# The opening of a one-core layer norm, linear attention and gated MLP kernel: all loads on one queue, wk transposed by DMA, tile 3 by another route

## The chip, the cores and the metric

The kernel runs on one core of a Trainium2 chip. The core has a matrix engine (TensorE, PE in the profile), three engines for elementwise work (VectorE, DVE; ScalarE, ACT; GpSimd, POOL) and an engine that here only issues transfers (SyncE, SP). Sixteen DMA engines move data. The metric is the device time of one execution in microseconds (us); lower is better.

## The reference

The input `x` has 2048 tokens of 512 values. It is normalized per token, goes through a linear attention of 32 heads of 16 and through a gated MLP of width 1792, and both results are added to `x`:

```python
xn = _layernorm(x, axis=-1)                      # (x - mean) / sqrt(var + 1e-5)
# attention
q, k, v = split(xn @ wqkv)                       # 32 heads of 16
pq, pk = q @ w_phi, k @ w_phi                    # per head, 16 x 16
phi = concat(softmax(p), softmax(-p))            # of pq and of pk
num = phi_q @ (phi_k^T v);  den = phi_q . sum(phi_k) + 1e-6
A = (num / den) @ wo
# gated MLP
B = ((xn @ w_gate) * (xn @ w_up)) @ w_down
return x + A + B
```

All arrays are bfloat16.

## The kernel before

The 2048 tokens are 16 tiles of 128 (`NT`), in four groups of four (`GT`). A token is a partition of `xall`; the normalized tile is needed transposed, as `xnT` (512 features in four blocks of 128 partitions, by token). Order on each engine is the order of the program text (`manual_schedule`, L92): an engine runs its instructions in that order and waits at each for its inputs.

**Loads (L75 to L89, L97).** All on SP's queue and in this order: tile 0 of x, tile 1, tiles 2 and 3, `wk` (the k columns of `wqkv`, rows on partitions), the first 256 columns of `wg` and `wu` (two units of the MLP), `wphi`, the next 640 columns of each (five units), tiles 4 to 7, the last 896 columns of each (seven units), tiles 8 to 15, `wd`, `wo`. The v columns `wv` go on ScalarE's own queue (L97), behind a one-element Exp (L96) that brings in the activation table.

**Opening (L328 to L357).** TensorE first runs ten products of zeros (`warm_up(10)`, L304). For tiles 0 to 3 VectorE takes statistics (`ln_sums`, L146) and aggregates them (L338), adds epsilon (L155), GpSimd raises to the power -1/2 (L157), and VectorE applies mean and scale (L162). The statistics of a tile stand ahead of the normalization of the tile before it. `lt(n)` transposes a normalized tile by four TensorE instructions into PSUM (L207), and ScalarE copies it to `xnT` (L208). `vproj(n)` makes the v product of a tile in four 512-wide matmuls (L235) and copies it out (L316); its argument `amid` puts the transposes of the next tile in the middle of it. `wk_transposes` (L217) turns `wk` into `wT2[:, 1]` by 16 TensorE transposes and two ScalarE copies (L222, L223), between the v products of tiles 1, 2 and 3. `make_bd` (L214, GpSimd) multiplies `wphi` by a block mask into `bd`, and `fold` (L229, L231) combines `wT2` and `bd` into `W1k`, the matrix that gives the projected k directly.

**Afterwards.** `ffn(1)` is one unit of the MLP, one of 14 blocks of 128 columns for a group of four token tiles: four `g` matmuls (L272), four `u` matmuls (L276), a ScalarE copy (L279) and a VectorE product (L280). It needs all four tiles of the group in `xnT`. Units are strewn between the other products so that TensorE always has work. The first units of group 0 alternate with the two halves of the fold of `W1k`; then follow the k features of tiles 0 to 3 (`kproj`, L319, which waits for `W1k`), `kv` sums, and the statistics of later tiles, which are put in as chores (`ln_block`, `chore`). The other tiles of `xnT` are transposed by DMA (L196), and the q half `wT2[:, 0]` by one DMA from DRAM (L379). Then comes attention (`attend`) and the output (`fin`).

**Buffers.** PSUM for products is six banks in rotation (`bank`), so a product waits until the bank six allocations earlier is read out. `hpool` has three large buffers, which `wk`, `wT2` and the `hT` of the groups take in turn.

Of the kernel before, what the change touches and what calls it, by code (L numbers as in the profile page):

```python
# [9 lines left out]
F32 = mybir.dt.float32  # L10
# [11 lines left out]
def kernel(  # L22
# [40 lines left out]
    wo = wpool.tile([P, DC, D], BF16)  # L63

    hpool = ctx.enter_context(tc.tile_pool(name="hpool", bufs=3))
    wk = hpool.tile([P, DC, D], BF16, name="wk", tag="h")
    wT2 = hpool.tile([P, 2, DC, D], BF16, name="wT2", tag="h")

    def dma_x(lo, hi):
        nc.sync.dma_start(out=xall[:, lo:hi, :], in_=x_view[:, lo:hi, :])  # L70

    def dma_cols(eng, w, src, lo, hi, at=0):
        eng.dma_start(out=w[:, :, lo - at:hi - at], in_=src[:, lo:hi].rearrange("(c p) f -> p c f", p=P))

    F1, F2 = 2 * P, 7 * P  # L75
    for lo, hi in ((0, 1), (1, 2), (2, 4)):
        dma_x(lo, hi)
    dma_cols(nc.sync, wk, A_wqkv, D, 2 * D, at=D)
    dma_cols(nc.sync, wg, B_w_gate, 0, F1)
    dma_cols(nc.sync, wu, B_w_up, 0, F1)  # L80
    nc.sync.dma_start(out=wphi[:], in_=A_w_phi.rearrange("(c h) d f -> (h d) c f", c=DC))
    dma_cols(nc.sync, wg, B_w_gate, F1, F2)
    dma_cols(nc.sync, wu, B_w_up, F1, F2)
# [10 lines left out]
    nc.vector.memset(zeros[:], 0.0)  # L94
    first = consts.tile([P, 1], BF16)
    nc.scalar.activation(out=first[:], in_=zeros[:, 0:1], func=AF.Exp, scale=1.0)  # L96
    dma_cols(nc.scalar, wv, A_wqkv, 2 * D, 3 * D, at=2 * D)  # L97
    ident = consts.tile([P, P], BF16)
    make_identity(nc, ident[:])
    mhalf = consts.tile([P, GT], F32)  # L100
# [38 lines left out]
    def bank(name, dt=F32, n=TT):  # L139
        return ps_s.tile([P, n], dt, name=name, tag="s")  # L140
# [9 lines left out]
        stats = ln_sums(n)  # L150
        nc.vector.bn_aggr(out=mv, in_=stats[:])

    def ln_rstd(mv, k):
        ve = lnpool.tile([P, GT], F32, name="ve")
        nc.vector.tensor_scalar(out=ve[:, 0:k], in0=mv[:, 0:k, 1], scalar1=EPS, scalar2=None, op0=ALU.add)  # L155
        rstd = lnpool.tile([P, GT], F32, name="rstd", bufs=GT)
        nc.gpsimd.tensor_tensor(out=rstd[:, 0:k], in0=ve[:, 0:k], in1=mhalf[:, 0:k], op=ALU.pow)  # L157
        return rstd

    def ln_apply(n, mean, rstd):  # L160
        xn = xnpool.tile([P, D], BF16, name="xn")
        nc.vector.tensor_scalar(out=xn[:], in0=xall[:, n, :], scalar1=mean, scalar2=rstd,  # L162
                                op0=ALU.subtract, op1=ALU.mult)
        xns[n] = xn

    def mv_tile():
# [10 lines left out]
    def ln_block(lo):  # L177
        mv = mv_tile()
        nb = lnpool.tile([P, GT], F32, name="nb", bufs=GT)
        rstd = []  # L180

        def scales():
            ve = lnpool.tile([P, GT], F32, name="ve4")
            nc.gpsimd.tensor_scalar(out=ve[:], in0=mv[:, :, 1], scalar1=EPS, scalar2=None, op0=ALU.add)
            r = lnpool.tile([P, GT], F32, name="rstd4", bufs=GT)
            nc.gpsimd.tensor_tensor(out=r[:], in0=ve[:], in1=mhalf[:], op=ALU.pow)
            nm = lnpool.tile([P, GT], F32, name="nm")
            nc.gpsimd.tensor_scalar(out=nm[:], in0=mv[:, :, 0], scalar1=-1.0, scalar2=None, op0=ALU.mult)
            nc.gpsimd.tensor_tensor(out=nb[:], in0=nm[:], in1=r[:], op=ALU.mult)
            rstd.append(r)  # L190

        def apply(i):
            xn = xnpool.tile([P, D], BF16, name="xn")
            nc.scalar.activation(out=xn[:], in_=xall[:, lo + i, :], func=AF.Identity,
                                 scale=rstd[0][:, i:i + 1], bias=nb[:, i:i + 1])
            nc.sync.dma_start(out=xnT[:, :, (lo + i) * P:(lo + i + 1) * P], in_=xn[:], transpose=True)  # L196

        for i in range(GT):
            chores.append(lambda i=i: ln_stats(lo + i, mv[:, i, :]))
        chores.append(scales)  # L200
        for i in range(GT):
            chores.append(lambda i=i: apply(i))

    def lt(n):
        tp = bank("tp", BF16).rearrange("p (c t) -> p c t", c=DC)
        for c in range(DC):
            nc.tensor.transpose(out=tp[:, c, :], in_=xns[n][:, c * P:(c + 1) * P], identity=ident[:])  # L207
        nc.scalar.copy(out=xnT[:, :, n * P:(n + 1) * P], in_=tp)  # L208

    bd = consts.tile([P, DC, 8, DH], BF16)  # L210

    def make_bd():
        bo, wp = BO[:], wphi[:]
        nc.gpsimd.tensor_tensor(out=bd[:], in0=_bcast_ap(bo, [bo.ap[0], [0, DC], [E1, 8], [1, DH]]),  # L214
                                in1=_bcast_ap(wp, [wp.ap[0], [DH, DC], [0, 8], [1, DH]]), op=ALU.mult)

    def wk_transposes(jp):  # L217
        tp = bank("tp", BF16, 2 * TT).rearrange("p (c t) -> p c t", c=DC)
        for i in range(2):
            j = jp * 2 + i  # L220
            for c in range(DC):
                nc.tensor.transpose(out=tp[:, c, i * P:(i + 1) * P], in_=wk[:, j, c * P:(c + 1) * P], identity=ident[:])  # L222
        nc.scalar.copy(out=wT2[:, 1, :, jp * 2 * P:(jp + 1) * 2 * P], in_=tp)  # L223

    def fold(qk, dst, js, copy=nc.scalar.copy):
        for j in js:
# [73 lines left out]
    def warm_up(k):  # L300
        for _ in range(k):
            nc.tensor.matmul(warm, lhsT=zeros[:, 0:P], rhs=zeros[:], start=True, stop=True)
# [3 lines left out]
    with tc.tile_pool(name="ps_k", bufs=1, space=PSUM) as ps_k:  # L306
        kvps = [ps_k.tile([P, 4, 4, E1], F32, name=f"kv{b}") for b in range(2)]
        phiks = {}

        def vproj(n, copy=nc.scalar.copy, amid=None):  # L310
            ps = bank("pv")
            proj(ps, n, wv, range(2))
            if amid is not None:
                amid()
            proj(ps, n, wv, range(2, DC))
            copy(out=vts[n % NV][:, :, :, 0:DH], in_=ps.rearrange("p (a b c) -> p a b c", a=8, b=4))  # L316

        def kproj(n):
            phiks[n] = features(n, W1k, "k")  # L319

        def kv(n):
            vt, phik = vts[n % NV], phiks[n]
            for gr in range(NG):
                nc.tensor.matmul(kvps[gr // 4][:, gr % 4, :, :].rearrange("p a b -> p (a b)"),  # L324
                                 lhsT=phik[:, gr, :], rhs=vt[:, gr, :, :].rearrange("p a b -> p (a b)"),
                                 start=(n == 0 and gr % 4 == 0), stop=(n == NT - 1 and gr % 4 == 3))

        mvs = [mv_tile() for n in range(GT)]  # L328
        rstds = []

        def first_apply(n):
            ln_apply(n, mvs[n][:, 0, 0:1], rstds[n][:, 0:1])

        for n in range(GT):
            stats = ln_sums(n)
            if n > 0:
                first_apply(n - 1)
            nc.vector.bn_aggr(out=mvs[n][:, 0, :], in_=stats[:])  # L338
            rstds.append(ln_rstd(mvs[n], 1))
        first_apply(GT - 1)  # L340
        make_bd()
        nc.gpsimd.tensor_tensor(out=M4[:], in0=BO[:, 0:4, :], in1=BO[:, 4:8, :], op=ALU.add)
        lt(0)
        warm_up(2)
        vproj(0, amid=lambda: lt(1))
        vproj(1, copy=nc.vector.tensor_copy, amid=lambda: lt(2))
        wk_transposes(0)
        vproj(2, copy=nc.vector.tensor_copy, amid=lambda: lt(3))
        wk_transposes(1)
        vproj(3, copy=nc.vector.tensor_copy)  # L350
        ffn(1)
        fold(1, W1k, (0, 1))
        ffn(1)
        fold(1, W1k, (2, 3))
        ffn(1)
        ln_block(4)
        ffn(1)  # L357
        chore(2)
        kproj(0)
        ffn(1)  # L360
        chore(2)
        ffn(1)
        chore()
        kproj(1)
        ffn(1)
        chore()
        ffn(1)
        kproj(2)
        chore()
        ffn(1)  # L370
        kv(0)
        chore()
        ffn(1)
        kproj(3)
        chore()
        ffn(1)
        kv(1)
        ffn(1)
        nc.sync.dma_start(out=wT2[:, 0, :, :], in_=A_wqkv[:, 0:D], transpose=True)  # L379
        for n in range(GT, NT):  # L380
            if n in (4, 8):
                ln_block(n + 4)
            vproj(n)
            kproj(n)
            chore(1 if n % GT < 2 else 0)
            ffn(1)
            kv(n - 2)
            chore((1, 2, 2, 2)[n % GT])
            if n >= 8 and n % 2 == 0:
                qproj((n - 8) // 2)  # L390
            if n == 6:
                fold(0, W1q, (0, 1))
            ffn(1)
            if n == 6:
                fold(0, W1q, (2, 3))
        ffn(1)
        kv(NT - 2)
        ffn(1)
        kv(NT - 1)
        for b in range(2):  # L400
            nc.vector.tensor_tensor(out=KV[:, 4 * b:4 * b + 4, :, :], in0=kvps[b][:],
                                    in1=_bcast_ap(M4[:], [M4[:].ap[0], [0, 4], [E1, 4], [1, E1]]), op=ALU.mult)
        qproj(4)
        ffn(1)
# [64 lines left out]
```

## Time and profile before

| what | value |
|---|---|
| median of 3 runs | 225.01 us (224.81 to 225.06) |
| profiled execution, its own time | 224.9 us |
| profiled execution, span from first to last instruction | 223.2 us |
| first v product starts (L235) | 6.33 us |
| four v products of tile 3 start | 12.05 us |
| first `g` product of the MLP starts (L272) | 12.93 us |
| VectorE idle before statistics, waiting for x | 2.2 us in 2 waits |
| last large load (`wo`) lands | 12.45 + 18.1 = 30.6 us |

Times inside the profile count from the start of the span. A timeline row gives start, length, engine, line, operation, the tile written and the tiles read, and, where the engine stood idle before, how long and for what. Some rows of the opening before:

```profile
2.99 0.69 DVE L146 BATCH_NORM_STATS2 stats<-xall 128x6 f32<-128x512 bf16 x1 [1.11 <-DMA xall<-in_A_x_dram]
...
4.79 0.41 DVE L162 TENSOR_SCALAR xn<-xall,mv,rstd 128x512 bf16<-128x512 bf16 x1
...
5.69 0.59 ACT L208 COPY xnT<-tp 128x512 bf16<-128x512 bf16 x1 [3.41 <-PE tp L207]
...
6.33 0.60 PE L235 MATMUL pv<-wv,xnT 128*128 128x512 bf16 x2 [0.25 <-ACT xnT L208]
6.61 0.69 DVE L146 BATCH_NORM_STATS2 stats<-xall 128x6 f32<-128x512 bf16 x1 [1.13 <-DMA xall<-in_A_x_dram]
```

The first column is the start, so ScalarE had been idle for 3.41 us when it copied the first transposed tile at 5.69, and VectorE waited 1.13 us for tiles 2 and 3 of x, until 6.61.

### The profile page before, as it was taken

To read this page: it belongs to the slowest core of one execution; us is meant where nothing else is said; L and a number is where in the kernel's file an instruction comes from. 1 tells how busy PE (TensorE), PEld (TensorE's weight loads), DVE (VectorE), ACT (ScalarE), POOL (GpSimd) and SP (SyncE) were. 2 spreads that over 40 slices of the span, in tenths; PEclk is the share of its full clock that TensorE was granted. 3 is DMA by queue.
4 is the path that set the end of the run, shared out by engine and by line. 5 is a ranking of instruction groups with operands and counts; after the bars stand their busy time and mean duration, and the time that the engine had idled before them with its cause. 6 is when DMAs were issued, how large, how long until landed. Compare 5 with 4: busy or idle time off the path is not lost.

```text
span 223.2 us, 3437 instructions
## 1 busy us (share of the span) xinstructions
PE 217.4 (97%) x1278; PEld 105.4 (47%) x1278; DVE 137.9 (62%) x237; ACT 90.3 (40%) x161; POOL 72.1 (32%) x59
## 2 busy tenths in 40 slices
PE   7799999999999999999999999999999999999994
PEld 2354444445444444444454444444444444444453
DVE  5634986586559875757679975097745746444321
ACT  2574575448955685646354122222222222100000
POOL 3310455336235663636315453014033033000000
PEclk9999999999999999999999999999999999999999
DMA  6999923501110224020203664314431431622301
GB/s 178 317 381 394 349 55 74 94 1 21 38 38 0 47 50 94 1 47 3 47 1 71 99 140 94 75 24 94 94 73 24 93 72 24 91 55 71 72 25 47
DMA packets 44481, 19.91 MB, mean 89 GB/s; under 512 B 35248, under 2 KB 44080, under 8 KB 44336
## 3 DMA queue, kind: packets, MB, share of 16 engines
q1 hardware_dynamic: 43936, 19.16, 34.8%
q10 hardware_dynamic: 528, 0.52, 0.8%
q8 instruction: 10, 0.16, 0.3%
q14 instruction: 7, 0.06, 0.1%
HBM read 9.19 MB, written 2.10 MB: 51 GB/s over the span
## 4 chain that ended last, share of the span: by engine, by line
PE 95%; DMA 2%; DVE 1%; SPq 0%; ACT 0%; issue 0%
PE fin L288 22%; PE u L276 22%; PE g L272 22%; PE fin L291 6%; PE k L235 6%; PE q L235 6%; PE pv L235 6%; DMA xall<-in_A_x_dram 2%; PE ab L412 2%; PE kv L324 2%; PE pq L229 1%; PE tp L222 0%; PE tp L207 0%; SPq L70 0%; DVE stats L146 0%; ACT xnT L208 0%
## 5 line engine op out<-in xcount | busy, mean ns | idle before, releaser
L276 PE MATMUL u<-xnT,wu 128*128 128x512 bf16 x224 | 57.5, 379 | 0.0
L272 PE MATMUL g<-xnT,wg 128*128 128x512 bf16 x224 | 57.5, 379 | 0.0
L280 DVE TENSOR_TENSOR hT<-u,g_sb 128x512 bf16<-128x512 f32 x56 | 37.1, 668 | 28.3 <-PE u L276 19.5
L247 DVE TENSOR_REDUCE sums<-e 128x64 f32<-128x1024 f32 x32 | 38.9, 1215 | 21.5 <-ACT e L244 21.5
L279 ACT CAST g_sb<-g 128x512 bf16<-128x512 f32 x56 | 32.9, 588 | 46.5 <-PE g L272 46.5
L288 PE MATMUL fin<-wd,hT 128*128 128x512 bf16 (+1 forms) x238 | 51.1, 366 | 0.0
L251 POOL TENSOR_TENSOR phiq<-e,rs 128x1024 bf16<-128x1024 f32 x16 | 30.9, 1932 | 61.5 <-DVE rs L249 53.2
L251 POOL TENSOR_TENSOR phik<-e,rs 128x1024 bf16<-128x1024 f32 x16 | 30.9, 1932 | 47.6 <-DVE rs L249 45.6
L276 PEld LDWEIGHTS <-wu 128*128 128x128 bf16 x224 | 21.9, 98 | 26.4
L288 PEld LDWEIGHTS <-hT 128*128 128x128 bf16 x238 | 23.0, 98 | 24.1
L272 PEld LDWEIGHTS <-wg 128*128 128x128 bf16 x224 | 21.1, 98 | 23.4
L235 PEld LDWEIGHTS <-xnT 128*128 128x128 bf16 x192 | 17.2, 97 | 18.7 <-ACT xnT L208 1.7
L294 DVE TENSOR_TENSOR o_sb<-fin,xall 128x512 bf16<-128x512 f32 (+1 forms) x17 | 11.2, 656 | 22.4 <-PE fin L291 22.4
L243 ACT ACTIVATE e<-q 128x512 f32<-128x512 f32 x16 | 9.5, 596 | 26.1 <-PE q L235 26.1
L249 DVE RECIPROCAL rs<-sums 128x64 f32<-128x64 f32 x32 | 17.7, 553 | 3.1
L235 PE MATMUL pv<-wv,xnT 128*128 128x512 bf16 x64 | 16.9, 379 | 0.6 <-ACT xnT L208 0.5
L291 PE MATMUL fin<-wo,oT 128*128 128x512 bf16 (+1 forms) x68 | 16.6, 366 | 0.0
L235 PE MATMUL k<-W1k,xnT 128*128 128x512 bf16 x64 | 16.4, 379 | 0.0
L235 PE MATMUL q<-W1q,xnT 128*128 128x512 bf16 x64 | 16.4, 378 | 0.0
L243 ACT ACTIVATE e<-k 128x512 f32<-128x512 f32 x16 | 9.6, 597 | 7.0 <-PE k L235 7.0
L316 ACT CAST vt<-pv 128x512 bf16<-128x512 f32 x13 | 7.7, 591 | 11.5 <-PE pv L235 11.5
L146 DVE BATCH_NORM_STATS2 stats<-xall 128x6 f32<-128x512 bf16 x16 | 10.7, 670 | 2.2 <-DMA xall<-in_A_x_dram 2.2
(50 smaller groups left out, 125.1 us busy)
## 6 DMA issues: line engine op xcount, KB each, us to landing
out_dram<-o_sb SPq DMA_DIRECT2D x15, 128.0 KB, 1.9
wd<-in_B_w_down_dram SPq DMA_DIRECT2D x1, 1792.0 KB, 17.5
xall<-in_A_x_dram SPq DMA_DIRECT2D x1, 1024.0 KB, 13.4
wg<-in_B_w_gate_dram SPq DMA_DIRECT2D x1, 896.0 KB, 8.5
wu<-in_B_w_up_dram SPq DMA_DIRECT2D x1, 896.0 KB, 11.4
wg<-in_B_w_gate_dram SPq DMA_DIRECT2D x1, 640.0 KB, 7.9
wu<-in_B_w_up_dram SPq DMA_DIRECT2D x1, 640.0 KB, 7.0
wv<-in_A_wqkv_dram ACTq DMA_DIRECT2D x1, 512.0 KB, 4.4
```

The source lines that it names most:

```text
L235: nc.tensor.matmul(ps, lhsT=xnT[:, j, n * P:(n + 1) * P], rhs=w[:, j, :], start=(j == 0), stop=(j == DC - 1))
L243: nc.scalar.activation(out=e[:, :, 0, :], in_=pfv, func=AF.Exp, scale=1.0)
L247: nc.vector.tensor_reduce(out=sums[:], in_=ev, axis=AX.X, op=ALU.add)
L249: nc.vector.reciprocal(out=rs[:].rearrange("p a b -> p (a b)"), in_=sums[:])
L251: nc.gpsimd.tensor_tensor(out=phi[:].rearrange("p g (x f) -> p (g x) f", f=DH), in0=ev, in1=rs[:].to_broadcast((P, 2 * H, DH)), op=ALU.mult)
L272: nc.tensor.matmul(gps, lhsT=wg[:, c, f * P:(f + 1) * P], rhs=xnT[:, c, T * TT:(T + 1) * TT], start=(c == 0), stop=(c == DC - 1))
L276: nc.tensor.matmul(ups, lhsT=wu[:, c, f * P:(f + 1) * P], rhs=xnT[:, c, T * TT:(T + 1) * TT], start=(c == 0), stop=(c == DC - 1))
L279: nc.scalar.copy(out=g_sb[:], in_=gps)
L280: nc.vector.tensor_tensor(out=hTs[T][:, f, :], in0=ups, in1=g_sb[:], op=ALU.mult)
L288: nc.tensor.matmul(ps, lhsT=hTs[T][:, f, t4 * P:(t4 + 1) * P], rhs=wd[:, f, lo:lo + w], start=(f == 0), stop=False)
L291: nc.tensor.matmul(ps, lhsT=oTs[n][:, c, :], rhs=wo[:, c, lo:lo + w], start=False, stop=(c == DC - 1))
L294: nc.vector.tensor_tensor(out=o_sb[:], in0=ps, in1=xall[:, n, lo:lo + w], op=ALU.add)
```

## The change

- **Loads.** Tiles 1, 2 and 3 of x come in one transfer behind tile 0. `wv` follows on SP's queue; ScalarE issues no transfer any more. Behind the first `wg` and `wu` columns stands one transposing DMA from DRAM that writes `wT2[:, 1]`. `wk`, its tile, its 16 TensorE transposes and their copies are gone.
- **Layer norm of tile 3.** ScalarE sums the tile (Identity with a sum output), GpSimd makes the negative mean, ScalarE sums the squared deviations (Square with a bias and a sum output), and GpSimd makes variance plus epsilon and the power. VectorE only applies them, ahead of tile 2.
- **Copies of tiles 0 and 1 to `xnT`** are made in two halves each. The two warm-up products after `lt(0)` are gone.
- **Order on TensorE.** v products of tiles 0, 1, 3, 2, then two units of the MLP, the first half of the fold, one unit, the second half, one unit. Before, a unit stood ahead of each half and two behind. From the second unit behind the fold on the order is as before.
- `ln_rstd` takes the engine for the addition of epsilon as an argument, and the later layer norm blocks use it with GpSimd, with the same operations as before.

```diff
     hpool = ctx.enter_context(tc.tile_pool(name="hpool", bufs=3))
-    wk = hpool.tile([P, DC, D], BF16, name="wk", tag="h")
     wT2 = hpool.tile([P, 2, DC, D], BF16, name="wT2", tag="h")
...
-    for lo, hi in ((0, 1), (1, 2), (2, 4)):
-        dma_x(lo, hi)
-    dma_cols(nc.sync, wk, A_wqkv, D, 2 * D, at=D)
+    dma_x(0, 1)
+    dma_x(1, 4)
+    dma_cols(nc.sync, wv, A_wqkv, 2 * D, 3 * D, at=2 * D)
     dma_cols(nc.sync, wg, B_w_gate, 0, F1)
     dma_cols(nc.sync, wu, B_w_up, 0, F1)
+    nc.sync.dma_start(out=wT2[:, 1, :, :], in_=A_wqkv[:, D:2 * D], transpose=True)
     nc.sync.dma_start(out=wphi[:], in_=A_w_phi.rearrange("(c h) d f -> (h d) c f", c=DC))
...
-    dma_cols(nc.scalar, wv, A_wqkv, 2 * D, 3 * D, at=2 * D)
...
-    def lt(n):
+    def lt(n, parts=1):
...
-        nc.scalar.copy(out=xnT[:, :, n * P:(n + 1) * P], in_=tp)
+        for c in range(0, DC, DC // parts):
+            nc.scalar.copy(out=xnT[:, c:c + DC // parts, n * P:(n + 1) * P], in_=tp[:, c:c + DC // parts, :])
...
-        for n in range(GT):
-            stats = ln_sums(n)
-            if n > 0:
-                first_apply(n - 1)
-            nc.vector.bn_aggr(out=mvs[n][:, 0, :], in_=stats[:])
-            rstds.append(ln_rstd(mvs[n], 1))
-        first_apply(GT - 1)
+        def first_rstd(n):
+            rstds[n] = ln_rstd(nc.vector, mvs[n], 1)
+        def first_aggr(n, stats):
+            nc.vector.bn_aggr(out=mvs[n][:, 0, :], in_=stats[:])
+            first_rstd(n)
+        last = GT - 1
...
+        nc.scalar.activation(out=junk[:], in_=xall[:, last, :], func=AF.Identity, accum_out=tot[:, 0:1])
+        nmean = lnpool.tile([P, 1], F32, name="nmean")
+        first_aggr(0, ln_sums(0))
+        st = ln_sums(1)
+        nc.gpsimd.tensor_scalar(out=nmean[:], in0=tot[:, 0:1], scalar1=-1.0 / D, scalar2=None, op0=ALU.mult)
+        nc.scalar.activation(out=junk[:], in_=xall[:, last, :], func=AF.Square, bias=nmean[:], accum_out=tot[:, 1:2])
+        first_apply(0)
+        first_aggr(1, st)
+        st = ln_sums(2)
+        first_apply(1)
+        nc.gpsimd.tensor_scalar(out=ml[:, 0, 1:2], in0=tot[:, 1:2], scalar1=1.0 / D, scalar2=EPS,
+                                op0=ALU.mult, op1=ALU.add)
+        rl = lnpool.tile([P, 1], F32, name="rl")
+        nc.gpsimd.tensor_tensor(out=rl[:], in0=ml[:, 0, 1:2], in1=mhalf[:, 0:1], op=ALU.pow)
+        first_aggr(2, st)
+        ln_apply(last, nmean[:], rl[:], op0=ALU.add)
+        first_apply(2)
...
-        lt(0)
-        warm_up(2)
-        vproj(0, amid=lambda: lt(1))
-        vproj(1, copy=nc.vector.tensor_copy, amid=lambda: lt(2))
-        wk_transposes(0)
-        vproj(2, copy=nc.vector.tensor_copy, amid=lambda: lt(3))
-        wk_transposes(1)
-        vproj(3, copy=nc.vector.tensor_copy)
-        ffn(1)
+        lt(0, parts=2)
+        vproj(0, amid=lambda: lt(1, parts=2))
+        vproj(1, copy=nc.vector.tensor_copy, amid=lambda: lt(3))
+        vproj(3, copy=nc.vector.tensor_copy, amid=lambda: lt(2))
+        vproj(2, copy=nc.vector.tensor_copy)
+        ffn(2)
         fold(1, W1k, (0, 1))
         ffn(1)
         fold(1, W1k, (2, 3))
-        ffn(1)
         ln_block(4)
         ffn(1)
```

More of the change, by code (lines that the diff above doesn't have):

```diff
@@ L151, in ln_stats, with ln_rstd @@
         nc.vector.bn_aggr(out=mv, in_=stats[:])
-    def ln_rstd(mv, k):
+    def ln_rstd(eng, mv, k):
         ve = lnpool.tile([P, GT], F32, name="ve")
-        nc.vector.tensor_scalar(out=ve[:, 0:k], in0=mv[:, 0:k, 1], scalar1=EPS, scalar2=None, op0=ALU.add)
+        eng.tensor_scalar(out=ve[:, 0:k], in0=mv[:, 0:k, 1], scalar1=EPS, scalar2=None, op0=ALU.add)
         rstd = lnpool.tile([P, GT], F32, name="rstd", bufs=GT)
@@ L158, in ln_rstd, with ln_apply @@
         return rstd
-    def ln_apply(n, mean, rstd):
+    def ln_apply(n, mean, rstd, op0=ALU.subtract):
         xn = xnpool.tile([P, D], BF16, name="xn")
         nc.vector.tensor_scalar(out=xn[:], in0=xall[:, n, :], scalar1=mean, scalar2=rstd,
-                                op0=ALU.subtract, op1=ALU.mult)
+                                op0=op0, op1=ALU.mult)
         xns[n] = xn
@@ L182, in scales @@
         def scales():
[L183 to L186, printed above, removed]
+            r = ln_rstd(nc.gpsimd, mv, GT)
             nm = lnpool.tile([P, GT], F32, name="nm")
@@ L215, in make_bd @@
                                 in1=_bcast_ap(wp, [wp.ap[0], [DH, DC], [0, 8], [1, DH]]), op=ALU.mult)
[L217 to L223, printed above, removed]
     def fold(qk, dst, js, copy=nc.scalar.copy):
@@ L328 @@
         mvs = [mv_tile() for n in range(GT)]
-        rstds = []
+        rstds = {}
         def first_apply(n):
             ln_apply(n, mvs[n][:, 0, 0:1], rstds[n][:, 0:1])
-        for n in range(GT):
-            stats = ln_sums(n)
-            if n > 0:
-                first_apply(n - 1)
+        def first_rstd(n):
+            rstds[n] = ln_rstd(nc.vector, mvs[n], 1)
+        def first_aggr(n, stats):
             nc.vector.bn_aggr(out=mvs[n][:, 0, :], in_=stats[:])
-            rstds.append(ln_rstd(mvs[n], 1))
@@ L340 @@
-        first_apply(GT - 1)
+            first_rstd(n)
+        last = GT - 1
+        junk = lnpool.tile([P, D], BF16, name="junk")
+        tot = lnpool.tile([P, 2], F32, name="tot")
+        ml = mvs[last]
+        nc.scalar.activation(out=junk[:], in_=xall[:, last, :], func=AF.Identity, accum_out=tot[:, 0:1])
[3 more added lines that the diff above has]
+        nc.gpsimd.tensor_scalar(out=nmean[:], in0=tot[:, 0:1], scalar1=-1.0 / D, scalar2=None, op0=ALU.mult)
```

## Prediction

> **What bounds the kernel.** First the page: busy shares, the slices, the chain that ended last.
>
> ```profile
> PE 217.4 (97%) x1278; PEld 105.4 (47%) x1278; DVE 137.9 (62%) x237; ACT 90.3 (40%) x161; POOL 72.1 (32%) x59
> ...
> PE   7799999999999999999999999999999999999994
> ...
> PE 95%; DMA 2%; DVE 1%; SPq 0%; ACT 0%; issue 0%
> ```
>
> TensorE sets the end. Next the busy time by stretches (us: busy and count of PE, PEld, DVE, ACT, POOL, clock, DMA share, GB/s), cut where the first gated unit's first product starts, 12.93.
>
> ```profile
> 1.24:12.93 11.69, 10.28 (x61) 4.61 (x62) 6.93 (x23) 5.67 (x9) 4.59 (x10) 1.00 0.97 293
> 12.93:215.00 202.07, 202.03 (x1179) 96.89 (x1178) 129.11 (x209) 84.18 (x153) 66.98 (x44) 1.00 0.34 80
> ```
>
> From 12.93 to 215 TensorE idles 0.04 us in 202, so what happens before 12.93 moves the end one for one, and nothing later takes it back unless a new wait appears. The edits all lie before; the mark is the start of that product. Now the chain of waits in time order (start, length, what).
>
> ```profile
> 1.71 4.88 DMA xall<-in_A_x_dram
> ...
> 6.61 0.69 DVE stats L146
> 7.31 0.33 DVE xn L162
> ...
> 8.11 0.59 ACT xnT L208
> ...
> 8.75 0.60 PE pv L235 x2
> ...
> 10.01 0.45 PE tp L222 x8
> ...
> 11.55 0.46 PE tp L222 x8
> 12.01 0.04 issue
> 12.05 1.04 PE pv L235 x4
> ```
>
> The opening hangs on the load of tiles 2 and 3, which lands at 1.71+4.88=6.59. VectorE's statistics of tile 2 start then, and tile 1's normalization stands behind them on VectorE. After that TensorE is nearly full, and 0.45+0.46=0.91 us of it is the 16 transposes of `wk`.
>
> **Loads.** Landing is issue start plus the median to landing: x0 0.79+2.2=2.99, x1 1.25+2.4=3.65, `wv` on ACT's queue 1.22+4.4=5.62, `wk` 8.48, first `wg`/`wu` columns 9.35 and 10.4, `wphi` 10.69, second `wg`/`wu` columns 12.35 and 14.13. The DMA view:
>
> ```profile
> wk<-in_A_wqkv_dram SPq DMA_DIRECT2D x1, 512.0 KB, 6.3
> ...
> wT<-in_A_wqkv_dram SPq DMA_TRANSPOSE x1, 4.4
> ```
>
> Tiles 1 to 3 are now one load of 384 KB issued at 1.25, with only x0 ahead. It can't land before x1 alone did (3.65) nor after 6.59, by when x0 to x3 and `wv` had all landed. By 1-us stretches, 246, 481, 811 and 1095 KB had moved by 3, 4, 5 and 6 us; its last byte is the 524th KB, at 4.15, and x0 landed 0.5 after its last byte. I take L=4.5. `wv` is then third on SP, the 1049th KB, at 5.85 plus lag; the same bytes had landed by 6.59 before. I take 6.5, later than 5.62.
>
> **VectorE, ScalarE, GpSimd.** Tile 3's statistics, aggregate and epsilon leave VectorE (0.69+0.18+0.15=1.02 us). ScalarE gets two passes over tile 3. None with a sum output is in the trace; the rows are 0.59 (128x512 copy) and 0.82 (128x512 with scale and bias tiles), so 0.7 and 0.75, with 0.2 more for reading each sum as upper bound. If Square needed a second table load, that is the 1.28 row; I give it nothing, since copies, Identity and Exp already share the one load. GpSimd gets two small operations at 0.24 and a power at 0.55.
> Step by step with L=4.5. VectorE: tile 1 statistics 4.5 to 5.2, and tile 0's normalization behind them 5.2 to 5.6 (it ran at 4.79; this is a loss); aggregate, epsilon, power, statistics of tile 2 (0.18, 0.15, 0.56, 0.69), tile 1 normalized by 7.15 against 7.62. ScalarE: Identity 4.5 to 5.2, GpSimd's mean to 5.5, Square to 6.3. Tile 0's transposes end at 6.05, but their copies wait behind Square: first half at 6.35. Half copies: 1024 columns took 1.01 and 512 took 0.59, so 256 about 0.38; the first product of tile 0 starts at 6.75 against 6.33. Two warm-up matmuls (0.43) leave, in a time in which TensorE waits anyway.
> What is queued: behind Square all later ScalarE copies; on GpSimd tile 1's power behind the mean (free at 5.5, its input comes at 6.0) and tile 2's behind tile 3's (done 7.5, input 7.55), so no loss; then the mask product `bd`.
>
> **TensorE.** A 512-wide product costs 0.216 (0.86 for four), a tile's four transposes 0.22, and 0.17 passes before their result is whole. Tile 0 first half 6.75; tile 1's transposes 7.2 (input 7.15); tile 0 second half to 7.85; tile 1 from 8.0; tile 3's transposes 8.45 (its normalization 7.6 to 8.0); tile 1 done 9.1. ScalarE: tile 1's copies 7.63 to 8.3, cast of tile 0's values to 8.87, tile 3's copy to 9.46. Tile 3 first half 9.5, tile 2's transposes 9.94, second half to 10.6, tile 2's copy to 10.95, its four products 11.0 to 11.86. No `wk` transposes stand between, nor their 1.01 copies, of which the last held `pv` until 12.05. The first gated product starts at about 11.9 against 12.93: **1.0 us earlier**. Of it 0.9 is the `wk` work. The late start (0.4) is repaid by tiles 2 and 3 coming 2 us earlier, and TensorE still waits some 0.4 twice, on the copies of tiles 3 and 2.
>
> **Is the cover there afterwards?** Two units now stand ahead of the first fold, one between the folds. Unit 2 starts 3.89 after the mark (3.46 of two units, 0.43 of a fold): `wg` columns needed at 15.8, `wu` at 16.7, `wT2` and `bd` at 15.4. The transposed load replaces 512 KB that took 8.48-6.59=1.9. Its other half, alone later:
>
> ```profile
> 39.00:40.00 1.00, 1.00 (x6) 0.42 (x5) 0.47 (x1) 0.43 (x1) 1.00 (x1) 1.00 0.74 101
> 40.00:41.00 1.00, 1.00 (x6) 0.48 (x5) 0.00 (x0) 0.66 (x3) 0.10 (x1) 1.00 1.05 143
> 41.00:42.00 1.00, 1.00 (x8) 0.43 (x6) 0.39 (x1) 1.00 (x3) 0.00 (x0) 1.00 1.25 281
> ```
>
> Those three columns move 525 KB in 3 us with the engines full, some 175 GB/s. Bounds for its time in the queue, T: 1.9 (as plain) and 4.4 (issue to landing alone); I take 3.0, for it starts with descriptors ready. Then everything behind lands 1.1 later than before: `wT2` 8.5+3.0=11.5, `wphi` 11.8, `bd` (1.08) 12.9, second `wg` 13.5, second `wu` 15.2. Slack is 1.5 at the tightest, so I cost the transfer at nothing; at 4.4 `wu` lands at 16.6, still just in time. Its issue holds SP 2.30 instead of 0.43, which puts `wphi`'s issue near 5.7 and the next near 6.3. The latter stood blocked until 7.09 before, so the queue does not run dry. Next on SP are the `xnT` transposes at 30.07; SP was free at 22.46. Tiles 4 to 7 land about 16.6, wanted at about 19.7. `W1k` casts (1.07 for two) have one unit, 1.73, before the first `k` product instead of two: enough.
>
> The Trainium skill, "Advanced Engine Details and Errata", X-Bar Transpose, says that such transfers are as fast as ordinary ones, at 350 to 400 GB/s; the rows above give 175. By the page T would be an estimated 1.4 and the second `wu` would land near 13.6; the total is the same. Against dropping the warm-up stands "TensorE: Matmul & The Clock Gate", Part 1 and Part 4: the array falls to half rate after an idle window of some 3.4 us, and transposes do not count fully as work. Warm-up weight loads here come every 0.43 until 4.5 and products every 0.216 after, and a gap of 0.74 at 6.93 did no harm; the new stretch without a plain product, 5.14 to 6.75, is half a window, so by the page also no fall.
>
> **Sum.** 1.0 off the profiled 224.9 (span 223.2 and 1.7 around it) is 223.9; off the median, 225.0-1.0=**224.0**. With everything else fixed the mark moves one for one with L: L=4.0 gives 223.5, L=5.0 224.5; the 0.2 for each sum output adds up to 0.4 more.
>
> **Rivals.**
> *Gain eaten in the opening* (16%). L near 5.3 (tile 0's normalization waits for all of x), or sum outputs at 0.2 each with `wv` near 7. The mark comes at 12.5 to 12.9: 224.6 to 225.0. For it: two things on the path do start later. Against: the bytes by 4.15.
> *The transposed load is slow in a full queue* (10%), the slower side. `wu`'s second columns land at 14.13-1.9+T. Before, unit 2 ended at 18.98 with both folds done; now 0.86 of products and 0.43 of fold follow the landing. So it decides from T=18.98-1.29-12.23=5.5 on. At T=6.5, 175 GB/s halved and a bit, the end moves to 226.0. For it: nearly all of the page's 35248 packets under 512 B are those of transposes. Against: 4.4 alone, issue included.
> *Half clock returns* (5%). 0.43 instead of 0.216 a product adds 2.2 over eight products and eight transposes (1.73+0.44), of which the two later waits hide 0.9: 224.0+1.3=225.3.
> *The forecast* (69%): 223.5 to 224.5.
>
> A measurement of this kernel can tell 0.2%, 0.45 us, from no change. The forecast with the upper edge taken off, and a little of the first rival, gives faster 0.69; same 0.17; slower 0.14. The range reaches from L=3.7 (223.2) past the eaten gain to 225.2.
>
> **What would show it.** Right: tile 1's statistics start at 4.2 to 4.9, the first `pv` product at 6.5 to 7.1, the first gated product at 11.5 to 12.4, and no wait on TensorE after it. Wrong: statistics after 5.3; an ACT table load beside Square; waits of the fold or of unit 2 for a DMA; products every 0.43 after 6.7.

## The result and the profile after

| what | before | after |
|---|---|---|
| median, 20 runs each | 225.05 us (224.81 to 225.45) | 225.93 us (224.64 to 226.28) |
| ratio, 95% interval | 1 | 1.0024 (1.0014 to 1.0035) |
| profiled execution, time / span | 224.9 / 223.2 us | 225.95 / 224.2 us |
| first `g` product of the MLP | 12.93 us | 14.03 us |

The changed kernel is slower, by 0.24% by the ratio and by 0.39% by the medians. Its 20 times fall into two groups with nothing between: six from 224.64 to 224.82 (middle 224.77) and fourteen from 225.70 to 226.28 (middle 225.96), 1.2 us apart. The kernel before has one group. The profiled execution of the changed kernel belongs to the upper one. All of its loss is made before the first gated product: that starts 1.10 later, and the span is 1.0 longer.

The page of the changed kernel, the lines that answer to those of before, and the granted clock in 40 slices of 5.6 us:

```profile
PE 216.4 (96%) x1236; PEld 105.0 (47%) x1260; DVE 137.0 (61%) x234; ACT 90.0 (40%) x165; POOL 72.7 (32%) x61
...
PEclk9799999999999999999999999999999999999999
...
PE 94%; DMA 2%; ACT 1%; issue 1%; DVE 0%; SPq 0%; POOL 0%
```

The second slice has a clock of 0.7. (TensorE shows 24 matmul records fewer than weight loads; those are records missing from the trace.) Busy time by stretches, in the columns of the prediction's table (busy and count of PE, PEld, DVE, ACT, POOL, then clock, DMA share, GB/s), shows where the clock fell. The changed kernel:

```profile
4.84:8.25 3.41, 1.35 (x9) 0.46 (x8) 2.51 (x8) 2.07 (x6) 1.48 (x4) 1.00 1.24 301
8.25:11.66 3.41, 3.41 (x16) 1.54 (x14) 0.83 (x2) 1.82 (x4) 0.93 (x3) 0.50 0.93 157
11.66:14.20 2.54, 2.29 (x14) 1.03 (x14) 1.39 (x2) 0.59 (x1) 1.06 (x2) 1.00 1.00 344
```

The same stretches before:

```profile
4.84:8.25 3.41, 2.30 (x16) 0.79 (x14) 2.21 (x8) 0.72 (x2) 0.83 (x2) 1.00 1.02 328
8.25:11.66 3.41, 3.16 (x31) 1.96 (x30) 2.00 (x7) 2.69 (x5) 1.71 (x3) 1.00 1.13 317
```

For 3.41 us TensorE ran at half rate, after a stretch of the same length in which it had been busy for 1.35. All of the half-rate stretch counts as busy, so the busy share does not show the loss. Now the chain of waits in time order:

```profile
1.25 4.25 DMA xall<-in_A_x_dram
...
5.52 0.73 ACT junk L334 x2
...
6.33 0.30 POOL nmean L339
...
6.66 0.81 ACT junk L340 x2
7.47 0.27 ACT xnT L205
...
7.79 0.63 PE pv L224 x2
...
8.84 1.71 PE pv L224 x4
...
10.97 1.28 PE pv L224 x4
...
12.52 0.59 ACT xnT L205
...
13.16 1.04 PE pv L224 x4
14.20 0.86 PE g L261 x4
```

Two things differ from what was foreseen. The load of tiles 1 to 3 lands at 5.50, and the chain hangs on it through ScalarE's two passes. And four v products take 1.71 (0.43 each) and not 0.86. The loads of the changed kernel (KB, us from issue to landing):

```profile
wv<-in_A_wqkv_dram SPq DMA_DIRECT2D x1, 512.0 KB, 5.9
...
xall<-in_A_x_dram SPq DMA_DIRECT2D x1, 384.0 KB, 4.2
...
wT<-in_A_wqkv_dram SPq DMA_TRANSPOSE x1, 7.7
```

`wv` lands at 1.71+5.9=7.6, the transposed weights at 3.28+7.7=11.0, which is 1.75 behind the first `wu` columns (2.73+6.5=9.23). TensorE waits for no load afterwards.

### The profile page after: what moved, and what is told of

It is laid out like the page before. It is cut to its first block, busy times and chain, and to the rows that moved or that the text cites. A ratio compares the mean times of both kernels' runs of the same rounds, so it can differ in the third digit from the quotient of the medians.

```text
span 224.2 us, 3380 instructions
## 1 busy us (share of the span) xinstructions
PE 216.4 (96%) x1236; PEld 105.0 (47%) x1260; DVE 137.0 (61%) x234; ACT 90.0 (40%) x165; POOL 72.7 (32%) x61
## 4 chain that ended last, share of the span: by engine, by line
PE 94%; DMA 2%; ACT 1%; issue 1%; DVE 0%; SPq 0%; POOL 0%
PE g L261 22%; PE u L265 21%; PE fin L277 21%; PE pv L224 7%; PE fin L280 6%; PE q L224 6%; PE k L224 6%; PE kv L313 2%; DMA xall<-in_A_x_dram 2%; PE ab L419 2%; PE pq L218 1%; PE tp L203 0%; ACT xnT L205 0%; ACT junk L340 0%; ACT junk L334 0%
## 5 line engine op out<-in xcount | busy, mean ns | idle before, releaser
L265 PE MATMUL u<-xnT,wu 128*128 128x512 bf16 x220 | 56.8, 379 | 0.1
L224 PE MATMUL pv<-wv,xnT 128*128 128x512 bf16 x62 | 17.7, 404 | 1.1 <-ACT xnT L205 1.0
L305 ACT CAST vt<-pv 128x512 bf16<-128x512 f32 x13 | 7.7, 591 | 11.5 <-PE pv L224 11.5
L145 DVE BATCH_NORM_STATS2 stats<-xall 128x6 f32<-128x512 bf16 x15 | 10.0, 668 | 2.5 <-DMA xall<-in_A_x_dram 2.5
```

What stands on the lines that cost most here:

```text
L224: nc.tensor.matmul(ps, lhsT=xnT[:, j, n * P:(n + 1) * P], rhs=w[:, j, :], start=(j == 0), stop=(j == DC - 1))
L265: nc.tensor.matmul(ups, lhsT=wu[:, c, f * P:(f + 1) * P], rhs=xnT[:, c, T * TT:(T + 1) * TT], start=(c == 0), stop=(c == DC - 1))
```

## The experiments

Each was run in five rounds beside the kernel before (medians 225.07 to 225.10 there). Edits are against the changed kernel unless it says otherwise.

**1. Warm-up products in the gaps**

```diff
-    warm_up(10)
+    warm_up(14)
...
         lt(0, parts=2)
+        warm_up(3)
         vproj(0, amid=lambda: lt(1, parts=2))
```

> Four more warm-up products ahead of tile 0's transposes and three behind them; nothing else differs from the changed kernel. Theory (half clock): the clock stays at 1.00 from 8.2 to 11.7, the two groups of times of the changed kernel (224.6 to 224.8 and 225.7 to 226.3) become one, at 224.6 to 224.9. Rival (the late x alone costs the time and the clock record means nothing): no difference, median 225.9. Third case: the products added get in the way of tile 0's transposes, 225 to 225.3, in one group.

Measured: 224.84 (224.71 to 225.16, 11 runs), ratio to before 0.9989 (0.9981 to 0.9998). One group, at the height of the lower one, as the theory had it. The two stretches with this edit:

```profile
4.84:8.25 3.41, 3.41 (x14) 1.30 (x13) 2.50 (x8) 2.17 (x6) 1.80 (x5) 1.00 1.24 306
8.25:11.66 3.41, 3.13 (x23) 1.49 (x22) 1.52 (x3) 1.73 (x5) 0.60 (x3) 1.00 0.91 156
```

Filling the first stretch keeps the clock in the second, although the added products compute nothing that is used. In the second stretch 23 matmuls of the same program started where 16 had. So the upper group is the clock, and it costs 225.96-224.77=1.2 us. (Nine of its fourteen runs list a mean clock of 0.990 to 0.992 and five 1.00; for those five it is inferred from the time.) The late x by itself makes the kernel no slower than before. The products can also be too many: in this profiled execution (225.16, the slowest of the eleven) x landed at 5.45, but the fourteen warm-up products, all at half rate, held tile 0's transposes until 7.18, and the first gated product came 7.78 behind x.

**2. x in three loads, and 3. `wv` on ScalarE's queue**

```diff
-    dma_x(1, 4)
+    dma_x(1, 2)
+    dma_x(2, 4)
```

> The changed kernel with x again as tile 0, tile 1, tiles 2 and 3; wv stays on SyncE's queue. Theory (the one 384 KB load is what comes late): tile 1's statistics start at 4.0 instead of 5.52, tile 0 is normalized near 4.8, TensorE's gap closes by itself and the clock holds; the wait moves to wv, which lands near 7.6; about 224.2. Rival (one queue fills slower than two whatever the pieces are): tile 1 comes by 4.3 but tiles 2 and 3 still at 5.5, and the gain is under 0.5: 225.4 or above, clock lost in some executions.

```diff
-    dma_cols(nc.sync, wv, A_wqkv, 2 * D, 3 * D, at=2 * D)
...
+    dma_cols(nc.scalar, wv, A_wqkv, 2 * D, 3 * D, at=2 * D)
```

> The changed kernel with wv on ScalarE's queue as before; x stays in two loads. Theory (384 KB in one piece is late): tiles 1 to 3 land no earlier than 5.5, later if wv takes half of the engines (to 6.5), and the time stays at 225.9 or goes to 226.5. Rival (two queues are what makes the first microseconds fast): they land by 5.0 and the time falls to 224.7 or below.

Measured: experiment 2 gave 225.29, scattered from 224.37 to 228.05 (12 runs). Tile 0 was normalized at 5.09 as hoped, but tiles 2 and 3 came at 5.56, the first product waited for `wv` until 8.1, and in the profiled execution (227.21) the products still came every 0.43 at 11.5:

```profile
1.24 4.45 PE L292 MATMUL warm<-zeros 128*128 128x512 bf16 x10 [1.24 <-DVE zeros L95]
...
9.33 1.91 PE L225 MATMUL pv<-wv,xnT 128*128 128x512 bf16 x4
...
11.46 1.92 PE L225 MATMUL pv<-wv,xnT 128*128 128x512 bf16 x4
```

Here the rate did not fall: the warm-up products come every 0.43 as well, and the full rate came only after 13 (the four transposes at 13.18 still took 0.63, against 0.39 at the full rate). The execution lists a mean clock of 1.00 all the same, so a listed 1.00 does not prove the full rate. With this in part of the runs, the experiment does not decide between its two cases; experiment 8 takes it up again. Experiment 3 gave 227.08 (226.57 to 227.49, 4 runs), above what either case gave: tiles 1 to 3 landed at 6.12 and `wv` at 1.22+6.3=7.5, and the clock fell too. So two queues do not bring the 384 KB piece sooner: from 3 to 5 us more bytes moved than in the changed kernel (412 against 367 KB), and x still came later. The rival there fell.

**4. The transposed weights alone, in the kernel before**

```diff
-    dma_cols(nc.sync, wk, A_wqkv, D, 2 * D, at=D)
...
+    nc.sync.dma_start(out=wT2[:, 1, :, :], in_=A_wqkv[:, D:2 * D], transpose=True)
...
-        wk_transposes(0)
...
-        wk_transposes(1)
```

> The kernel before with one part of the change alone: the k half of wT2 by transposing DMA in the same place as in the changed kernel, no wk and no transposes on TensorE. Theory (the loss is in the loads and the clock, the transposed load itself is sound): the first gated product comes 0.8 to 0.9 earlier, 224.1 to 224.3. Rival (a transposing load in a full queue holds up what is behind it): TensorE waits for a weight load in the units behind the fold, 225.0 or above.

Measured: 225.03 (224.60 to 225.60, 11 runs), ratio 0.9997 (0.9988 to 1.0005). Both expectations fail: nothing is gained, and no unit waits for a weight load. The timeline of this kernel shows why (start, length, and in brackets the idle time before and its releaser):

```profile
10.17 0.41 DVE L161 TENSOR_SCALAR xn<-xall,mv,rstd 128x512 bf16<-128x512 bf16 x1 [0.67 <-POOL rstd L156]
...
10.95 0.39 PE L206 MATMUL tp<-ident,xn 128*128 128x128 bf16 x4
...
11.37 0.59 ACT L207 COPY xnT<-tp 128x512 bf16<-128x512 bf16 x1 [0.92 <-PE tp L206]
...
12.01 1.04 PE L226 MATMUL pv<-wv,xnT 128*128 128x512 bf16 x4 [0.25 <-ACT xnT L207]
```

Tile 3 is normalized at 10.17, and with no `wk` work left its products still start at 12.01, against 12.05 before. The layer norm chain behind tiles 2 and 3 was as long as TensorE's work; the 0.91 us of transposes lay in the chain of waits with another chain close beside it. A part is the load: tiles 2 and 3 came at 6.86 in this execution, 0.25 later than before, and from there to the products of tile 3 it took 5.15 against 5.44. With x at the old time some 0.3 of the 0.91 would have shown, an estimate from these two executions.

**5. The transposed weights issued later** (with the warm-up products of experiment 1)

```diff
-    nc.sync.dma_start(out=wT2[:, 1, :, :], in_=A_wqkv[:, D:2 * D], transpose=True)
...
     dma_cols(nc.sync, wg, B_w_gate, F1, F2)
+    nc.sync.dma_start(out=wT2[:, 1, :, :], in_=A_wqkv[:, D:2 * D], transpose=True)
```

> The changed kernel with the seven extra warm-up products (so that the clock holds) and with the transposing load issued behind the second wg columns instead of ahead of wphi. Theory (starting that load empties the engines for about 1 us, between 3.0 and 4.0, while x is still coming): no dip of the rate below 190 GB/s between 3 and 5, tiles 1 to 3 land by 4.9 instead of 5.5, the first gated product 0.5 to 0.7 earlier than with the load in its place, 224.2 to 224.4. Rival (one queue with 3 KB rows is slow by itself): the dip stays, x at 5.4 or later, 224.8.

Measured: 224.87 (224.74 to 225.08, 11 runs). The theory falls and the rival's three signs are there: the dip, x after 5.4, and 224.8 to 224.9. The rates by stretches, first of the changed kernel, then of this one:

```profile
3.00:4.00 1.00, 1.00 (x4) 0.38 (x3) 0.93 (x3) 0.00 (x0) 0.00 (x0) 1.00 0.69 132
4.00:5.00 1.00, 1.00 (x4) 0.30 (x2) 0.06 (x1) 0.00 (x0) 0.58 (x1) 1.00 0.91 235
```

```profile
3.00:4.00 1.00, 1.00 (x4) 0.37 (x3) 0.83 (x2) 0.00 (x0) 0.00 (x0) 1.00 0.63 152
4.00:5.00 1.00, 1.00 (x4) 0.39 (x3) 0.20 (x2) 0.00 (x0) 0.58 (x1) 1.00 0.90 222
```

Before, those stretches moved 235 and 330 GB/s. The dip is there with the transposing load issued only at 5.94, and x lands at 5.51 all the same. With the clock held the first gated product starts at 12.95, which is 7.44 behind the landing of x.

**6. Only the two warm-up products that the change dropped**

```diff
         lt(0, parts=2)
+        warm_up(2)
         vproj(0, amid=lambda: lt(1, parts=2))
```

> The changed kernel with only the two warm-up products put back that it dropped after tile 0's transposes. If their removal lost the clock: one group at 224.7 to 224.9. If the late x lost it (1.3 us without work ahead of tile 0's transposes): two groups again, the slow one at 225.7 to 226.3 holding half of the runs or more.

Measured: 224.89; ten runs from 224.57 to 225.18 and two at 225.97 and 226.03. Neither case alone: two products bring the share in the upper group from 14 of 20 to 2 of 12, and do not abolish it. With five or seven products added in the gaps (experiments 1, 5, 7, 8) none of 44 runs is above 225.2. (The kernel before is not quite safe either: one of its 116 runs in all took 227.11, with a mean clock of 0.992.) Here x landed at 5.60 and the first gated product started at 13.04, again 7.44 later.

**7. Tile 3 back on VectorE** (with the warm-up products of experiment 1; tiles 2 and 3 in their old order)

```diff
-        nc.scalar.activation(out=junk[:], in_=xall[:, last, :], func=AF.Identity, accum_out=tot[:, 0:1])
...
-        ln_apply(last, nmean[:], rl[:], op0=ALU.add)
+        for n in range(GT):
+            st = ln_sums(n)
+            if n > 0:
+                first_apply(n - 1)
+            first_aggr(n, st)
+        first_apply(GT - 1)
```

> The changed kernel with the seven extra warm-up products and with tile 3's statistics back on VectorE, tiles 2 and 3 in their old order. If the ScalarE route earns its place: statistics of tiles 2 and 3 come one behind the other, the last v products start 0.6 to 0.9 later, 225.4 to 225.7 against 224.84. Rival (it costs as much as it saves, since tile 0's copies wait for Square): 224.7 to 225.0.

Measured: 224.76 (224.55 to 225.03, 11 runs), ratio 0.9983 (0.9975 to 0.9992). The rival holds: the ScalarE route earns nothing. In the profiled execution x landed at 5.79, and tile 0's first copy still began earlier than in the changed kernel (x at 5.50). This kernel, then the changed one:

```profile
7.29 0.65 ACT L205 COPY xnT<-tp 128x256 bf16<-128x256 bf16 x2 [5.01 <-PE tp L203]
```

```profile
7.29 0.19 ACT L340 ACTIVATION_READ_ACCUMULATOR junk<-xall,nmean 128x1 f32 x1
7.38 0.62 ACT L205 COPY xnT<-tp 128x256 bf16<-128x256 bf16 x2
```

There the copy starts when TensorE has transposed; here it stands behind Square and the 0.19 that reading the sum takes. From x to the first gated product it is 13.04-5.79=7.25, against 7.44.

**8. Three loads of x, late transposed weights, five warm-up products behind tile 0's transposes**

> The changed kernel with x in three loads, the transposing load behind the second wg columns, and five warm-up products after tile 0's transposes. Theory (dip and one 384 KB piece both delay the opening): tile 0 normalized near 4.8, wv landed by 7.0, the first gated product near 12, 223.8 to 224.1, in one group. Rival (wv at 7.6 to 8.1 on a single queue is the new bound): 224.3 to 224.5.

Measured: 224.83 (224.40 to 225.10, 11 runs), ratio 0.9987 (0.9978 to 0.9995). The edits are the loads of 2 and 5, without the warm-up products of experiment 1, and `warm_up(5)` where experiment 6 has two. Tiles 2 and 3 landed at 5.06 and tile 0 was normalized at 4.87, but its products waited for `wv` until 7.77. The rival's mechanism, at a time above its range.

**9. The kernel before with VectorE's order changed**

```diff
+        first_aggr(0, ln_sums(0))
+        st = ln_sums(1)
+        first_apply(0)
+        first_aggr(1, st)
+        first_apply(1)
+        first_aggr(2, ln_sums(2))
+        first_aggr(3, ln_sums(3))
+        first_apply(2)
+        first_apply(3)
```

> The kernel before with one thing changed: on VectorE tile 1 is normalized ahead of tile 2's statistics (which wait for the load), and tile 3's statistics come ahead of tile 2's normalization. Theory (the opening before is bound by the layer norm chain behind tiles 2 and 3, with wk's 16 transposes and two 1.01 copies close behind): 0.1 to 0.4 earlier, 224.7 to 225.0. If wk's work does not matter at all, the whole 0.7 shows: 224.4.

Measured: 225.30 (224.97 to 225.56, 11 runs), ratio 1.0005 (0.9988 to 1.0021). A miss: no gain. In the profiled execution tile 1's normalization waited for its power until 6.80 and so held tile 2's statistics until 7.13, later than the 6.61 of before. But tile 0 of x came at 3.63 there, against 2.99 in the profiled execution of before with the same loads. In experiment 11, with this order and tile 0 at 3.00, the two times are 6.17 and 6.50. So the order gained nothing in these runs, and whether it costs anything by itself is not shown.

**10. That order, `wk` by DMA, three warm-up products; 11. the same with `wv` on SyncE behind x; 12. the same with `wphi` behind the transposed weights.** Experiment 10 is the kernel before with the order of 9, the edit of 4 (behind the second `wg` columns), all copies in halves, and this sequence:

```diff
         lt(0)
-        warm_up(2)
+        warm_up(3)
         vproj(0, amid=lambda: lt(1))
         vproj(1, copy=nc.vector.tensor_copy, amid=lambda: lt(2))
-        wk_transposes(0)
-        vproj(2, copy=nc.vector.tensor_copy, amid=lambda: lt(3))
-        wk_transposes(1)
+        lt(3)
+        vproj(2, copy=nc.vector.tensor_copy)
         vproj(3, copy=nc.vector.tensor_copy)
-        ffn(1)
+        ffn(2)
```

> The kernel before with VectorE's order as in e9, wk by the transposing load (behind the second wg columns), copies to xnT in halves, tile 3's transposes ahead of tile 2's v products, three warm-up products instead of two, two units ahead of the first fold; wv stays on ScalarE's queue. Theory: taking wk off TensorE pays only once the layer norm chain is shorter; first gated product at 11.8 to 12.2 instead of 12.93, 223.9 to 224.3, in one group. Rival (the loads land later with another mix behind them, tiles 2 and 3 at 6.9 or more): 224.5 to 224.8.

> e10 with wv third on SyncE's queue behind x. Theory (one queue fills slower, wv comes at 7.6 to 7.8): tiles 2 and 3 land at 5.0 to 5.5 instead of 6.6, but the first v product moves from 6.2 to 7.8, and from there TensorE is nearly full: first gated product at 12.0 to 12.3, 224.0 to 224.4, 0 to 0.3 slower than e10. Rival (the queue does not matter): as e10 within 0.1.

> e11 with wphi loaded behind the transposed weights, so that GpSimd's mask product bd (1.07) no longer runs beside VectorE's normalization of tile 3, which took 1.16 instead of 0.41 in e11. Theory (the two hinder each other): normalization of tile 3 back to 0.41, first gated product 0.6 to 0.75 earlier than in e11, 223.6 to 223.9. Rival (bd then comes too late for the fold): TensorE waits for bd near 15, 224.3 or above. A wait of tile 3 on the copies would leave a part of the gain only: 224.0.

Measured: 10 gave 225.08, ten runs from 224.63 to 225.29 and two at 226.64 and 226.96 with the clock lost; 11 gave 224.36 (223.73 to 224.66, 6 runs), ratio 0.9963 (0.9950 to 0.9976); 12 gave 223.92 (223.76 to 224.24, 5 runs), ratio 0.9944 (0.9930 to 0.9958). Experiment 10 missed its forecast. Experiment 11 was expected to be a little slower than 10 and is 0.7 faster. In the two profiled executions tile 0 of x was there at 3.00 with one queue and at 3.84 with two, tile 2's statistics began at 6.50 and 7.33, and TensorE waited 0.39 for `wv`, until 7.13, on the one queue. Experiment 10 is also the one of the two that lost the clock. How much of the 0.7 is the queue is open: over all profiled executions tile 0 came at 2.99 to 3.84 with two queues (before, 3, 4, 9, 10) and at 2.96 to 3.31 with one (nine others), so the one queue brought it more evenly, and not always sooner. Experiment 11 showed a collision besides. GpSimd's mask product and VectorE's normalization of tile 3 in experiment 11:

```profile
9.29 1.07 POOL L214 TENSOR_TENSOR bd<-BO,wphi 128x512 bf16<-128x512 bf16 x1
9.36 1.16 DVE L161 TENSOR_SCALAR xn<-xall,mv,rstd 128x512 bf16<-128x512 bf16 x1 [0.44 <-POOL rstd L156]
```

And in experiment 12, where `wphi` lands later:

```profile
9.50 0.41 DVE L161 TENSOR_SCALAR xn<-xall,mv,rstd 128x512 bf16<-128x512 bf16 x1 [0.44 <-POOL rstd L156]
...
14.33 1.08 POOL L214 TENSOR_TENSOR bd<-BO,wphi 128x512 bf16<-128x512 bf16 x1 [4.86 <-DMA wphi<-in_A_w_phi_dram]
```

The normalization takes 0.41 again and the first gated product starts at 12.16 (12.53 in 11). Of the 0.75 on tile 3, 0.37 shows: in that execution the products of tile 0 waited for `wv` until 7.83, 0.70 later than in 11, and from there to 12.16 TensorE was busy for 4.29 of 4.33 us. This version beats both: 1.2 us below the kernel before, which ran beside it, and 2.0 below the changed one, which did not.

## Why the prediction was wrong

**What sets the end.** Right. A shift before the mark at 12.93 moves the end one for one: +1.10 at the mark, +1.05 in the two profiled executions' own times.

**The landing of x.** Mis-sized: "I take L=4.5" was 5.50, in every variant with the 384 KB piece 5.45 or later. The bytes were counted off the rows of before, which had two queues at work; with one, the three stretches from 2 to 5 us moved 253, 132 and 235 KB where before had 224, 235 and 330. The 5.5 is close to the 5.3 at which the prediction's first rival had the gain eaten. By the prediction's own rule, one for one with L, it takes the whole gain and gives 225.0; with the clock held the runs gave 224.84 and 224.87 (experiments 1 and 5). It also opens 1.3 us without work on TensorE ahead of tile 0's transposes.

**From x to the first gated product.** Right to 0.05: 11.9-4.5=7.4 foreseen, 7.44 in experiments 5 and 6 (7.78 in experiment 1, where the warm-up products stood in the way). The steps agree too, so this is not luck: in experiment 5 the first product came 2.26 behind x (6.75-4.5=2.25 foreseen) and the products of tile 2 came 6.57 behind it (11.0-4.5=6.5). The sum reads of 0.19 were within their bound, and the half copies took 0.35 to 0.38, as estimated.

**"Of it 0.9 is the `wk` work".** Wrong, by experiment 4: alone it gives 0.0, and some 0.3 if the later x of that execution is taken off. It was covered by the layer norm chain, which the prediction's own step list has, but did not run without the other edits.

**The route over ScalarE.** Foreseen as what lets tile 3 overtake; by experiment 7 it is worth nothing, 224.84 with it and 224.76 without. The wait of tile 0's copies behind Square was named, and not weighed against the gain.

**The transposed load.** T was taken as 3.0; it landed 1.75 behind the load ahead of it, below the lower bound of 1.9. Its issue held SP for 5.73, not 2.30, so that `wphi` was issued at 9.07 and not near 5.7. Costing it at nothing was right even so, and the rival with a slow load fell. The second `wg` and `wu` columns landed at 14.4 and 16.0, 0.8 to 0.9 later than foreseen, and still ahead of need.

**The clock.** This rival was the mechanism of the loss and had 5%. Its price, 1.3 us, was near the 1.2 measured, but it was worked out for L=4.5. The step that failed is "the new stretch without a plain product, 5.14 to 6.75, is half a window, so by the page also no fall". With x at 5.50 that stretch ran from 5.32 to 7.79, 2.47 us with four transposes in it, and 14 of 20 runs are in the upper group. The Trainium skill ("TensorE: Matmul & The Clock Gate", Part 1) speaks of an idle window. Here 1.35 us of work in 3.41 did not save the clock, while 2.30 did (the kernel before). The two other executions whose trace shows the fall had 1.24 (experiment 3) and 1.74 (experiment 10):

```profile
5.81:9.22 3.41, 1.24 (x11) 0.76 (x12) 2.71 (x9) 2.07 (x6) 1.86 (x5) 1.00 1.18 263
9.22:12.64 3.42, 3.42 (x12) 1.22 (x11) 1.16 (x3) 1.82 (x4) 0.40 (x2) 0.50 0.92 182
```

```profile
8.20:11.61 3.41, 1.74 (x13) 0.66 (x13) 2.86 (x8) 1.49 (x5) 2.55 (x4) 1.00 1.17 290
11.61:15.03 3.42, 3.42 (x12) 1.26 (x10) 1.04 (x2) 0.65 (x2) 0.00 (x0) 0.50 0.99 287
```

Experiment 6 kept the full rate after a stretch with 1.64:

```profile
4.21:7.62 3.41, 1.64 (x10) 0.53 (x8) 1.88 (x6) 1.60 (x5) 1.43 (x3) 1.00 1.00 304
7.62:11.04 3.42, 2.90 (x18) 1.28 (x19) 2.03 (x6) 2.19 (x6) 1.25 (x3) 1.00 1.15 192
```

Where the page and the runs differ the measurement decides: such a window need not be empty, and busy time alone gives no sharp limit. The length of the half-rate time, 3.41 us in all three, and the free-running window of that page agree with these traces: the half rate begins at 8.25, 9.22 and 11.61. That would account for two groups of one program; no run here shows it, for one execution of each kernel was traced.

Together: -1.0 foreseen, +1.0 for x, +1.1 for the clock gives +1.1 for the profiled execution; measured +1.05. For the lower group the first two give 0.0 and the times -0.3; no trace of it was kept. Of the prediction's signs of being wrong two came: statistics of tile 1 at 5.52, and products every 0.43 after 6.7.

What stays open: why the queue delivers so slowly from 3 to 4 us. It is not the transposing load (experiment 5), and a second queue by itself does not bring the piece sooner (experiment 3). Nor is it the piece alone: from 3 to 5 us one queue moved 300 to 374 KB with x in two loads and 347 to 386 KB with x in three, and two queues moved 412 KB (experiment 3) and 462 to 565 KB (before, 4, 9, 10). With three loads the slow stretch comes from 4 to 5 us, at 125 to 193 GB/s (experiments 2, 8, 11, 12).

## What to carry to other kernels

Where several chains run side by side, an item in the chain of waits is worth what is left when the next chain is put in its place; take it out alone and see before counting it. One profiled execution is one draw: with the same loads tile 0 of x came at 2.99 and at 3.63 (before and experiment 9). A landing time can't be read off the rate of another mix of queues and pieces, and a load that gathers small pieces makes the first wait for the last. In an opening where TensorE waits anyway, products that compute nothing are cheap insurance, as long as they end before the work behind them is ready: their absence does not show in any wait, only in the clock column and in two groups of times.

## What the runs showed of the hardware that was not expected

- Stretches of 3.41 us with TensorE busy for 1.24, 1.35 and 1.74 were followed by 3.41 us at clock 0.50 (experiment 3, the changed kernel, experiment 10); after 1.64 (experiment 6) and 2.30 (before) it stayed at 1.00. The clock column shows 1.00 also in the first 4.8 us of the changed kernel, where warm-up products still come every 0.43, and in experiment 2 up to 13 us.
- A VectorE pass of 0.41 (128x512 bf16, two per-token operands) took 1.16 beside a 1.07 GpSimd product of the same size (experiments 10 and 11). A VectorE cast out of PSUM, 0.69, was not stretched inside such a product (changed kernel, 11.84).
- A transposing load of 512 KB in a full queue landed 1.75 behind the load ahead of it; the same from DRAM later took 4.4 from issue in the kernel before.
- ScalarE takes 0.63 and 0.72 for 128x512 with a sum output, and 0.19 more for reading each sum.
